# Filter rows of a spectral mixer: even rows read backwards by DMA instead of turned on TensorE

## The chip, the cores and the metric

The kernel runs on one core of a Trainium2 chip. The metric is the device time of one execution in microseconds, as the median of several runs. The engines named below are TensorE (PE, with its weight loads as PEld), VectorE (DVE), ScalarE (ACT), GpSimd (POOL, unused here) and SyncE (SP), whose instruction stream issues nearly all DMAs of this kernel.

## The reference

Two branches read the same `x` of shape (1, 2048, 512), and a gate mixes them.

```python
def _A_ref(x, w_r, w_i):                      # spectral filter
    X = rfft2(x)                              # over (2048, 512), 257 columns kept
    X = X * (w_r + 1j * w_i)                  # filter: 2048 x 257
    return irfft2(X, s=(2048, 512)).astype(bf16)

def _B_ref(x, w1, b1, w2, b2):                # MLP over the token axis
    h = layernorm(x)
    u = gelu(einsum("bsd,sf->bdf", h, w1) + b1)      # f = 1792
    y = einsum("bdf,fs->bds", u, w2) + b2
    return y.transpose(0, 2, 1)

g = sigmoid((x * gate_w).sum(-1))
return g * A + (1 - g) * B
```

Inputs, tables and output are bfloat16; sums are kept in float32 in PSUM.

## The kernel before

**The transform.** The 2048-point transform along the tokens is split by four: DVE adds and subtracts quarters of `x`, PE multiplies by cosine and sine tables (`ta`, lines 509 to 516), and ACT copies the result to the tile `X` in SBUF. A frequency index k from 0 to 255 sits on each partition, the even ones in half `lt` = 0 of the tiles and the odd ones in half `lt` = 1; the four blocks of 512 frequencies and the mirrored ones stand in the free dimension. DVE finishes the token transform (`radix4`, lines 538 to 571), PE transforms along the 512 columns (`fb`, lines 618 to 625), ACT copies to the tile `B` (line 628), and DVE multiplies by the filter (`mul`, line 777) and combines (lines 782 to 791). Then everything runs backwards: an inverse radix-4 step on DVE, the matmuls `i1` (lines 838 to 845), folds on DVE (lines 861 to 874), the matmuls `i3` (lines 913 to 917) and the folds per output tile (lines 937 to 941).

**The filter in SBUF.** The tile `W` has the shape [128, component, lt, e, slot, 258]: the component is real or imaginary, e is one of four blocks of 512 rows, slot 0 holds row 512e + k, and slot 1 holds the mirrored row 2048 - 512e - k. The mirrored rows run downwards in the source as the partition goes up. For the odd rows, DMAs read them downwards (line 425). For the even rows they are loaded upwards into a tile `wt` (lines 419 to 423), and PE turns the partitions round with a reversed identity `flip` as the weights (`wf`, line 706; line 716 does column 256); ACT copies the result into `W` (lines 710 and 719). The even row k = 0 is a special case with rows of its own. `wprep` (lines 726 to 730) halves one row and prepares the sums for the edge columns; it is the first instruction of DVE that needs all of both components of `W`.

**The MLP.** First layer: 14 column tiles of `w1` times 16 token tiles, matmul by matmul (`m1`, line 656), then a gelu on ACT (line 670). Second layer: 16 output tiles j with 14 matmuls each (`m2`, line 932). The weights of the first layer lie in `wa` and two `wb` buffers; those of the second layer (seven loads of 1 MB, line 889) take over these buffers when they are free. These matmuls fill PE wherever the transform has nothing for it.

**The order of the work.** Every step is a task with an engine, an estimated duration, a priority and, for a DMA, a number of bytes. A planner (class `Plan`, lines 170 to 233) plays the tasks through with these estimates: whenever an engine is free, it takes the ready task with the smallest priority number. For a task with bytes, lines 222 to 225 move a common DMA clock on:

```python
if best.nbytes:
    dma_free = max(dma_free, now + best.dur + 1.0) + best.nbytes / 350e3
    end = dma_free + 0.4
    clock[eng] = max(clock[eng], dma_free - 5.0)
```

The planned times serve for nothing but the order: each engine's instructions are emitted in it, and every engine, SP too, works through its own list strictly in that order. The real waits are semaphores between the instructions that touch the same data.

**The loads that matter here.** SP issues the first four column loads of `wb`, then the gate weights, `ld_W(0)` (18 DMAs), the second four loads of `wb`, `ld_W(1)` (18 DMAs), the inverse table `ti`, the table `tg`, and the loads of `w2`. A row of the filter is 257 values, 514 bytes.

Of the kernel before, what the change touches and what calls it, by code (L numbers as in the profile page):

```python
# [34 lines left out]

def make_tables():
# [10 lines left out]
    for r in range(4):  # L47
        s = 4 * p + r
        for n, k0 in enumerate((0, 2)):
            th = ang(s, k0 + 4 * np.arange(64), S)  # L50
            ta[:, r, n * 128:n * 128 + 64] = np.cos(th)
            ta[:, r, n * 128 + 64:n * 128 + 128] = -np.sin(th)
        ta[:, r, 64] = alt
# [5 lines left out]
        k = np.where(p < 64, 4 * p, 2 + 4 * (p - 64))  # L59
        o, w = ti_at(r)  # L60
        v = ti[:, o:o + w]
        if r % 2:
            sg = np.where(p < 64, 1.0, -1.0)[:, None]
# [6 lines left out]
            v[0, 2:4] = alt * (0.5 ** 0.5 if r == 1 else -(0.5 ** 0.5))  # L70
            th = ang(1 + 4 * (p ^ 96), s, S)
            v[:, 4] = -np.sin(th)
            v[:, 5] = np.cos(th)
            v[:, 6] = np.sin(th)
            ti[:, o:o + w] = v.reshape(P, w)
        else:
            s5 = np.append(s, 512)
            for lt, kk in enumerate((k, 1 + 4 * (p ^ 96))):
                th = ang(kk, s5, S)
                c, n = np.cos(th), -np.sin(th)  # L80
                if lt == 0:
                    n[0, 0:P] = 0.0 if r == 0 else -alt
# [4 lines left out]
    ti[0, 2816:2945] = np.append(alt, 1.0)  # L87
# [174 lines left out]
def kernel(  # L262
# [150 lines left out]
    def ld_W(comp):  # L413
        v = wsrc[comp].rearrange("(e c k) l -> c e k l", e=4, k=4)
        z = wsrc[comp].rearrange("(v u w) l -> w u v l", v=4, u=2)

        def emit():
            W, u = t["W"][:, comp], t["wt"][:, comp]
            dma(u[64:127, :, 0:257], v[65:128, :, 0, :])
            dma(u[0:64, :, 0:257], v[64:128, :, 2, :])  # L420
            dma(u[127:128, 0:2, 0:257], z[0:1, 1, 2:4, :])
            dma(u[127:128, 2, 0:257], wsrc[comp][1536:1537, :])
            dma(u[127:128, 3, 0:257], wsrc[comp][0:1, :])
            for e in range(4):
                dma(W[:, 1, e, 1, 0:257], v[:, 3 - e, 3, :].rearrange("(o i) l -> o i l", o=4)[:, ::-1])
# [150 lines left out]
    def sp0():  # L576
        V.tensor_copy(t["sp"][:], t["X"][:, 0, :, :, :, 0])
# [25 lines left out]
    add("DVE", 0.15, lambda: V.tensor_copy(t["X"][:, 0, :, :, :, 0], t["fx"][:]), reads=["fx"],  # L603
# [94 lines left out]
    for comp in range(2):  # L698
        for lt in (0,):
            for a in range(2):  # L700
                tag = ("fa", "fb")[a]

                def wf(comp=comp, lt=lt, a=a, tag=tag):
                    pw = t["pw", comp, lt, a] = ps([P, 2, L], F32, tag, 2)
                    for i in range(2):
                        T.matmul(pw[:, i], lhsT=t["flip"][:], rhs=t["wt"][:, comp, 3 - 2 * a - i, 0:L], start=True, stop=True)
                add("PE", mm(256, 256), wf, reads=[("wt", comp), "flip"], writes=[("pw", comp, lt, a)], prio=5, alloc=[tag])

                def wfe(comp=comp, lt=lt, a=a):
                    A.copy(t["W"][:, comp, lt, 2 * a:2 * a + 2, 1, 0:L], t["pw", comp, lt, a][:])  # L710
                add("ACT", act(512), wfe, reads=[("pw", comp, lt, a)], writes=[("W~", comp, lt)], prio=3, free=[tag])

    def wfn():
        pw = t["pwn"] = ps([P, 4, 2], F32, "fa", 2)
        for e in range(4):
            T.matmul(pw[:, e], lhsT=t["flip"][:], rhs=t["wt"][:, :, 3 - e, 256], start=True, stop=True)
    add("PE", mm(*[4] * 4), wfn, reads=[("wt", 0), ("wt", 1), "flip"], writes=["pwn"], prio=5, alloc=["fa"])
    wtk = [("W~", comp, 0) for comp in range(2)]
    add("ACT", 0.3, lambda: A.copy(t["W"][:, :, 0, :, 1, 256], t["pwn"][:].rearrange("p e k -> p k e")),
        reads=["pwn"], writes=wtk, prio=3, free=["fa"])  # L720

    pbk = [("pb", lt, e, c) for lt in range(2) for e in range(4) for c in range(2)]

    def wprep():
        W, pm = t["W"], t["wpm"]
        V.tensor_scalar_mul(W[0:1, :, 0, 0, :, 0:257], W[0:1, :, 0, 0, :, 0:257], 0.5)
# [4 lines left out]
    add("DVE", 0.8, wprep, reads=[], writes=[("W", 0), ("W", 1), "wpm"] + wtk, prio=1)  # L731


    for lt in range(2):
# [8 lines left out]
        if lt == 0:  # L743
            def nyq():
                pz = sb([1, 1280], F32, "X")
                na = pz[:, 0:1024].rearrange("p (i v l) -> p i v l", i=2, v=2)
                nn = t["nn"] = pz[:, 1024:1280].bitcast(BF16).rearrange("p (v l) -> p v l", v=2)
                wn, v = t["wn"], t["B"][0:1, 0, 0, 2:4, :]
# [4 lines left out]
                V.tensor_mul(nn[:, :, 0], t["c0"][0:1, 0, 0, 1, :], wn[:, 0, 0:257:256])  # L753
# [18 lines left out]
        for comp in range(2):  # L772
# [5 lines left out]
            add("DVE", tt(4096), mul, reads=["xs", ("W", comp), ("W~", comp, lt)], writes=[("pp", "st")[comp]], prio=pr)  # L778
# [236 lines left out]
```

## Time and profile before

| what | value |
|---|---|
| median of 3 runs | 134.28 us (133.79 to 134.64) |
| the profiled execution | 134.46 us, span 132.6 us, granted clock 1.0 |
| PE busy | 124.6 us, 94% of the span |
| DVE busy | 115.3 us, 87% |
| ACT busy | 80.5 us, 61% |
| DMA | 23.18 MB, 175 GB/s mean over the span |
| SP issues `ld_W(0)` | from 21.70 to 34.66 us |
| SP issues `ld_W(1)` | from 37.37 to 51.05 us |
| last `m1` matmul ends, first `m2` matmul starts | about 70.4 us |

The profile shows one execution. Times in it count from the start of the span; the 1.86 us between the span and the execution's time lie outside it. A group of instructions stands with its line, engine, tiles and mean duration; "idle before" is the time that an engine waited, with the instruction or DMA that released it. The DMA share is the mean busy share of the core's 16 DMA engines, so that 0.25 is the work of four of them.

### The profile page before, as it was taken

The page shows a single profiled execution, that of the slowest core. Times are in us where ns is not written, and L with a number is a line of the kernel's source. Part 1 is how long each engine was busy: PE and PEld are TensorE (multiplying, and loading weights), DVE is VectorE, ACT ScalarE, POOL GpSimd, SP SyncE. Part 2 cuts the span into 40 slices and gives each one's busy share as a digit, 9 for nine tenths or more (in the row PEclk, how much of TensorE's full clock was granted, in tenths as well). Part 3 has the DMA queues.
Part 4 walks back from the last instruction along what each step waited for, and adds up shares of the span by engine and source line. Part 5 has one row for each costly group of instructions (what it writes and reads, how often), then busy time and mean ns, then how long its engine had stood idle before and what let it go on. Part 6 is the DMA issues. An engine that isn't in the chain of part 4 may idle for free.

```text
span 132.6 us, 2193 instructions
## 1 busy us (share of the span) xinstructions
PE 124.6 (94%) x769; PEld 70.7 (53%) x783; DVE 115.3 (87%) x295; ACT 80.5 (61%) x155; POOL 0.2 (0%) x4
## 2 busy tenths in 40 slices
PE   6749999999999999999999999999999999999991
PEld 2234464545544566744445544556865766655590
DVE  2987999999999997389999999999598599999841
ACT  4036699999999999972222016235994857755200
POOL 0000000000000000000000000000000000000000
PEclk9999999999999999999999999999999999999999
DMA  4899999925499565999964930000000003034031
GB/s 133 245 370 394 393 380 371 321 60 134 90 309 342 96 134 131 337 373 413 421 253 72 420 146 2 0 2 5 0 0 0 5 0 158 23 135 161 2 119 40
DMA packets 17350, 23.18 MB, mean 175 GB/s; under 512 B 1446, under 2 KB 14780, under 8 KB 17340
## 3 DMA queue, kind: packets, MB, share of 16 engines
q1 hardware_dynamic: 16780, 22.39, 49.8%
q10 hardware_dynamic: 560, 0.66, 1.6%
q8 instruction: 6, 0.10, 0.3%
q14 instruction: 4, 0.03, 0.1%
HBM read 20.93 MB, written 2.10 MB: 174 GB/s over the span
## 4 chain that ended last, share of the span: by engine, by line
PE 80%; DVE 10%; DMA 6%; SPq 1%; issue 1%
PE acc L932 35%; PE acc L656 25%; DMA x<-in_A_x_dram 6%; DVE stats L462 4%; PE fb L656 3%; PE fa L838 1%; PE fb L838 1%; PE fa L624 1%; PE fb L624 1%; SPq L303 1%; DVE mv L463 1%; DVE gl L495 1%; DVE st L494 1%; PE fa L513 1%; DVE nmr L477 1%
## 5 line engine op out<-in xcount | busy, mean ns | idle before, releaser
L932 PE MATMUL acc<-gl,wb 128*128 128x512 bf16 (+1 forms) x123 | 30.5, 373 | 0.3
L656 PE MATMUL acc<-h,wb 128*128 128x512 bf16 x124 | 28.8, 379 | 0.2
L932 PE MATMUL acc<-gl,wa 128*128 128x512 bf16 (+1 forms) x94 | 23.2, 372 | 0.1
L932 PEld LDWEIGHTS <-wb 128*128 128x128 bf16 x144 | 14.9, 114 | 10.7 <-DMA wb<-in_B_w_dram 0.6
L952 ACT ACTIVATE x<-acc,ombb,omg 128x512 bf16<-128x512 f32 x14 | 10.7, 778 | 15.5 <-PE acc L932 15.4
L656 PEld LDWEIGHTS <-wb 128*128 128x128 bf16 x128 | 12.4, 97 | 13.5
L656 PE MATMUL acc<-h,wa 128*128 128x512 bf16 x62 | 16.8, 379 | 1.2 <-DVE stats L462 0.7
L932 PEld LDWEIGHTS <-wa 128*128 128x128 bf16 x108 | 11.7, 114 | 8.5
L656 PEld LDWEIGHTS <-wa 128*128 128x128 bf16 x96 | 9.1, 98 | 10.3 <-DMA wa<-in_B_w_dram 0.9
L670 ACT ACTIVATE gl<-acc,b1f 128x512 bf16<-128x512 f32 x12 | 8.5, 708 | 9.6 <-PE acc L656 9.6
L462 DVE BATCH_NORM_STATS2 stats<-x 128x6 f32<-128x512 bf16 x16 | 10.8, 673 | 2.8 <-DMA x<-in_A_x_dram 2.8
L519 ACT CAST X<-fa 128x512 bf16<-128x512 f32 x16 | 8.8, 583 | 3.9 <-PE fa L516 3.8
L486 ACT ACTIVATE h<-x,nmr,rstd 128x512 bf16<-128x512 bf16 x13 | 9.8, 805 | 1.2 <-DVE nmr L477 1.2
L684 ACT ACTIVATE x<-x 128x512 bf16<-128x512 bf16 x16 | 10.2, 672 | 0.0
L923 ACT ACTIVATE eo<-fa,g 128x512 bf16<-128x512 f32 x8 | 5.5, 688 | 6.7 <-DVE x L958 5.0
L656 PE MATMUL fb<-h,wa 128*128 128x512 bf16 x31 | 9.0, 379 | 0.0
L513 PE MATMUL fa<-rot,gl 128*128 128x256 bf16 x16 | 4.3, 272 | 2.1 <-DMA rot<-dft_ta 2.1
L353 PE MATMUL fa<-xp 128*128 128x512 bf16 x13 | 4.4, 514 | 1.2 <-DVE xp L314 1.2
L923 ACT ACTIVATE eo<-fb,g 128x512 bf16<-128x512 f32 x8 | 5.5, 686 | 0.0
L958 DVE TENSOR_TENSOR x<-x,eo 128x512 bf16<-128x512 bf16 x14 | 5.4, 418 | 0.0
L628 ACT CAST B<-fb 128x512 bf16<-128x512 f32 x8 | 5.2, 651 | 0.0
L628 ACT CAST B<-fa 128x512 bf16<-128x512 f32 x8 | 5.1, 639 | 0.0
(170 smaller groups left out, 227.3 us busy)
## 6 DMA issues: line engine op xcount, KB each, us to landing
wb<-in_B_w_dram SPq DMA_DIRECT2D x8, 512.0 KB
wb<-in_B_w_dram SPq DMA_DIRECT2D x4, 1024.0 KB
wa<-in_B_w_dram SPq DMA_DIRECT2D x3, 1024.0 KB
wa<-in_B_w_dram SPq DMA_DIRECT2D x3, 768.0 KB
x<-in_A_x_dram SPq DMA_DIRECT2D x3, 512.0 KB
out_dram<-x SPq DMA_DIRECT2D x3, 512.0 KB
rot<-dft_ti SPq DMA_DIRECT2D x1, 736.5 KB
rot<-dft_ta SPq DMA_DIRECT2D x4, 160.0 KB
```

The source lines that it names most:

```text
L462: V.bn_stats(out=t["stats"][:, j, :], in_=t["x"][:, j // 4, j % 4, :])
L486: add("ACT", act(512, 2), lambda j=j: A.activation(t["h"][:, j // 4, j % 4, :], t["x"][:, j // 4, j % 4, :], ActF.Identity, bias=t["nmr"][ ...
L513: T.matmul(pa[:, 1], lhsT=w(2), rhs=ta[:, 256:512], start=True, stop=False)
L519: add("ACT", act(512), lambda r=r, dq=dq: A.copy(t["X"][:, :, r, :, dq, :], t["pa", r, dq][:]), reads=[("pa", r, dq)], writes=[("X", r, dq ...
L628: A.copy(t["B"][:, lt, e, 2 * c:2 * c + 2, :].rearrange("p s (i b) -> p s i b", b=4), t["pb", lt, e, c][:].rearrange("p s b i -> p s i b"))
L656: T.matmul(t["u", ft][:], lhsT=w[:, j // 4, j % 4, c * P:(c + 1) * P], rhs=t["h"][:, j // 4, j % 4, :], start=(j == jorder[0]), stop=(j == ...
L670: gelus.append(add("ACT", act(512, 1), lambda ft=ft: A.activation(t["gl"][:, ft, :], t["u", ft][:], ActF.Gelu_apprx_tanh, bias=t["b1f"][:, ...
L684: A.activation(t["x"][:, q, r, :], t["x"][:, q, r, :], ActF.Copy, accum_out=t["glog"][:, 4 * q + r:4 * q + r + 1])
L923: A.activation(t["eo", j][:], t["i3", j][:], ActF.Copy, scale=t["g"][:, j:j + 1])
L932: T.matmul(t["y", j, n][:, cs], lhsT=w[:, o, 512 * q + r:512 * q + 512:4], rhs=t["gl"][:, ft, cs], start=(ft == 0), stop=(ft == NFT - 1))
L952: A.activation(tbuf(j).rearrange("p h d -> p (h d)"), t["y", j, 0][:], ActF.Identity, bias=t["ombb2"][:, j:j + 1], scale=t["omg"][:, j:j + 1])
L958: V.tensor_add(o, o, t["eo", j][:])
```

## The change

The mirrored even rows are read downwards by DMA straight into `W`. For this the even frequencies are renumbered: partition 32q + i now holds k = 250 + 2q - 8i (modulo 256), that is one residue modulo 8 in each run of 32 partitions. The tables `ta` and `ti` follow, and row k = 0 moves from partition 0 to partition 96. The tile `wt`, the turning matmuls and their copies go. Per component there are now 20 DMAs in `ld_W`: for each o of four an even load in four downward runs, a mirrored load of 32 partitions (31 for o = 3), a single-row load, the odd load in four downward runs as before, and the odd forward load as before. The two DMAs that put the special rows over partition 96 become a task of their own with a later priority. The planner's figures for the loads change with it, and the tile `ze` gets memory of its own instead of that of `h`.

```diff
+KE = (250 + 2 * (np.arange(P) // 32) - 8 * (np.arange(P) % 32)) % 256
...
         def emit():
-            W, u = t["W"][:, comp], t["wt"][:, comp]
-            dma(u[64:127, :, 0:257], v[65:128, :, 0, :])
-            dma(u[0:64, :, 0:257], v[64:128, :, 2, :])
-            dma(u[127:128, 0:2, 0:257], z[0:1, 1, 2:4, :])
-            dma(u[127:128, 2, 0:257], wsrc[comp][1536:1537, :])
-            dma(u[127:128, 3, 0:257], wsrc[comp][0:1, :])
-            for e in range(4):
-                dma(W[:, 1, e, 1, 0:257], v[:, 3 - e, 3, :].rearrange("(o i) l -> o i l", o=4)[:, ::-1])
+            W, src = t["W"][:, comp], wsrc[comp]
+            tiny_ = [(W[96:97, 0, 1:3, 1, 0:257], z[0:1, 0:2, 3, :]), (W[96:97, 0, 0, 1, 0:257], src[0:1, :]),
+                     (W[96:97, 0, 3, 1, 0:257], src[1280:1281, :]), (t["wn"][96:97, comp, 0:257], src[1024:1025, :])]
             for o in range(4):
+                dma(W[:, 0, o, 0, 0:257], src[512 * o + 2:512 * o + 258, :].rearrange("(i q z) l -> q z i l", q=4, z=2)[:, 0, ::-1])
+                dma(W[32 * o + o // 3:32 * o + 32, 0, :, 1, 0:257], y[32 + o // 3:64, ::-1, 6 - 2 * o, :])
+                dma(*tiny_[o])
+                dma(W[:, 1, o, 1, 0:257], v[:, 3 - o, 3, :].rearrange("(o i) l -> o i l", o=4)[:, ::-1])
                 dma(W[32 * o:32 * o + 32, 1, :, 0, 0:257], v[96 - 32 * o:128 - 32 * o, :, 1, :])
-            dma(W[1:64, 0, :, 0, 0:257], v[1:64, :, 0, :])
-            dma(W[64:128, 0, :, 0, 0:257], v[0:64, :, 2, :])
+
+        def special():
             for i in range(2):
-                dma(W[0:1, 0, 2 * i:2 * i + 2, 0, 0:257], z[0:1, i, 0:2, :])
-            dma(t["wn"][:, comp, 0:257], wsrc[comp][1024:1025, :])
-        return emit
+                dma(t["W"][96:97, comp, 0, 2 * i:2 * i + 2, 0, 0:257], z[0:1, i, 0:2, :])
+        return emit, special

     for comp in range(2):
-        add("SP", 9.0 - 2 * comp, ld_W(comp), writes=[("W", comp), ("wt", comp)], prio=17 + 8 * comp, nbytes=300000, after=[a0])
+        emit, special = ld_W(comp)
+        add("SP", 8.0, emit, writes=[("W", comp)], prio=17 + 8 * comp, nbytes=1100000, after=[a0])
+        add("SP", 1.0, special, writes=[("W", comp)], prio=24 + 5.5 * comp, nbytes=4112)
...
-                T.matmul(pa[:, 0, :, 0:64], lhsT=w(0), rhs=ta[:, 0:128], start=True, stop=True)
-                T.matmul(pa[:, 0, :, 64:128], lhsT=w(1), rhs=ta[:, 128:256], start=True, stop=True)
+                T.matmul(pe[:, :, :, 1], lhsT=w(0), rhs=ta[:, 0:128], start=True, stop=True)
+                T.matmul(pe[:, :, :, 0], lhsT=w(1), rhs=ta[:, 128:256], start=True, stop=True)
...
-                        T.matmul(pw[:, i], lhsT=t["flip"][:], rhs=t["wt"][:, comp, 3 - 2 * a - i, 0:L], start=True, stop=True)
-                    A.copy(t["W"][:, comp, lt, 2 * a:2 * a + 2, 1, 0:L], t["pw", comp, lt, a][:])
-            T.matmul(pw[:, e], lhsT=t["flip"][:], rhs=t["wt"][:, :, 3 - e, 256], start=True, stop=True)
-    add("ACT", 0.3, lambda: A.copy(t["W"][:, :, 0, :, 1, 256], t["pwn"][:].rearrange("p e k -> p k e")),
...
-        V.tensor_scalar_mul(W[0:1, :, 0, 0, :, 0:257], W[0:1, :, 0, 0, :, 0:257], 0.5)
+        V.tensor_scalar_mul(W[96:97, :, 0, 0, :, 0:257], W[96:97, :, 0, 0, :, 0:257], 0.5)
...
-                dma(t["s9"][0:8], t["B"][0:1, 0].rearrange("p e (c v) l -> p (e c) (v l)", c=2))
+                dma(t["s9"][0:8], t["B"][96:97, 0].rearrange("p e (c v) l -> p (e c) (v l)", c=2))
...
-                        t["ze"] = sb([P, 2, 2, 2, 2, L], BF16, "h")
+                        t["ze"] = sb([P, 2, 2, 2, 2, L], BF16, "ze")
```

More of the change, by code (lines that the diff above doesn't have):

```diff
@@ L48, in make_tables @@
         s = 4 * p + r
-        for n, k0 in enumerate((0, 2)):
-            th = ang(s, k0 + 4 * np.arange(64), S)
+        for n in range(2):
+            kk = KE.reshape(2, 2, 32)[:, 1 - n].reshape(64)
+            th = ang(s, kk, S)
             ta[:, r, n * 128:n * 128 + 64] = np.cos(th)
             ta[:, r, n * 128 + 64:n * 128 + 128] = -np.sin(th)
-        ta[:, r, 64] = alt
+        ta[:, r, 96] = alt
         th = ang(s, 1 + 4 * (p ^ 96), S)
@@ L57, in make_tables @@
         ta[:, r, 512:640] = -np.cos(th)
-        k = np.where(p < 64, 4 * p, 2 + 4 * (p - 64))
+        k = KE
         o, w = ti_at(r)
@@ L62, in make_tables @@
         if r % 2:
-            sg = np.where(p < 64, 1.0, -1.0)[:, None]
+            sg = np.where(k % 4 == 2, -1.0, 1.0)[:, None]
             th = ang(k, s, S)
@@ L69, in make_tables @@
             v[:, 3] = -sg * np.sin(th)
-            v[0, 2:4] = alt * (0.5 ** 0.5 if r == 1 else -(0.5 ** 0.5))
+            v[96, 2:4] = alt * (0.5 ** 0.5 if r == 1 else -(0.5 ** 0.5))
             th = ang(1 + 4 * (p ^ 96), s, S)
@@ L81, in make_tables @@
                 if lt == 0:
-                    n[0, 0:P] = 0.0 if r == 0 else -alt
+                    n[96, 0:P] = 0.0 if r == 0 else -alt
                 u = v[:, 256 * lt:256 * lt + 256]
@@ L86, in make_tables @@
                     u[:, P] = c[:, P] if lt == 0 else -n[:, P]
-    ti[0, 2816:2945] = np.append(alt, 1.0)
+    ti[96, 2816:2945] = np.append(alt, 1.0)
     tb = np.zeros((P, 3, 4, 64))
@@ L322, in alloc_first @@
         t["W"] = sb([P, 2, 2, 4, 2, WL], BF16, "W")
-        t["wn"] = sb([1, 2, WL], BF16, "wn")
+        t["wn"] = sb([P, 2, WL], BF16, "wn")
         t["ta"] = sb([P, 4, 640], BF16, "rot")
-        t["wt"] = sb([P, 2, 4, WL], BF16, "wt")
         t["wpm"] = sb([P, 2, 2, 4, 2], F32, "wpm")
@@ L414, in ld_W @@
         v = wsrc[comp].rearrange("(e c k) l -> c e k l", e=4, k=4)
+        y = wsrc[comp].rearrange("(e c k) l -> c e k l", e=4, k=8)
         z = wsrc[comp].rearrange("(v u w) l -> w u v l", v=4, u=2)
         def emit():
[L418 to L425 removed]
+            W, src = t["W"][:, comp], wsrc[comp]
+            tiny_ = [(W[96:97, 0, 1:3, 1, 0:257], z[0:1, 0:2, 3, :]), (W[96:97, 0, 0, 1, 0:257], src[0:1, :]),
+                     (W[96:97, 0, 3, 1, 0:257], src[1280:1281, :]), (t["wn"][96:97, comp, 0:257], src[1024:1025, :])]
             for o in range(4):
+                dma(W[:, 0, o, 0, 0:257], src[512 * o + 2:512 * o + 258, :].rearrange("(i q z) l -> q z i l", q=4, z=2)[:, 0, ::-1])
+                dma(W[32 * o + o // 3:32 * o + 32, 0, :, 1, 0:257], y[32 + o // 3:64, ::-1, 6 - 2 * o, :])
+                dma(*tiny_[o])
+                dma(W[:, 1, o, 1, 0:257], v[:, 3 - o, 3, :].rearrange("(o i) l -> o i l", o=4)[:, ::-1])
                 dma(W[32 * o:32 * o + 32, 1, :, 0, 0:257], v[96 - 32 * o:128 - 32 * o, :, 1, :])
[L428 to L429 removed]
+        def special():
             for i in range(2):
[L431 to L433 removed]
+                dma(t["W"][96:97, comp, 0, 2 * i:2 * i + 2, 0, 0:257], z[0:1, i, 0:2, :])
+        return emit, special
     for comp in range(2):
[L436 removed]
+        emit, special = ld_W(comp)
+        add("SP", 8.0, emit, writes=[("W", comp)], prio=17 + 8 * comp, nbytes=1100000, after=[a0])
+        add("SP", 1.0, special, writes=[("W", comp)], prio=24 + 5.5 * comp, nbytes=4112)
         if comp == 0:
@@ L511, in fa @@
                 ta = t["ta"][:, r, :]
+                pe = pa[:, 0].rearrange("p c (h o i) -> p c h o i", h=2, o=2)
                 w = lambda k: t["xf", r][:, k, dq * P:(dq + 1) * P]
@@ L576, in sp0 @@
     def sp0():
-        V.tensor_copy(t["sp"][:], t["X"][:, 0, :, :, :, 0])
+        V.tensor_copy(t["sp"][:], t["X"][:, 0, :, :, :, 96])
     dk = [("D", r) for r in range(4)]
@@ L602 @@
                dk + ([] if lt else ["sp"]), [("Z", lt, 0), ("Z", lt, 1)], pr, False)
-    add("DVE", 0.15, lambda: V.tensor_copy(t["X"][:, 0, :, :, :, 0], t["fx"][:]), reads=["fx"],
+    add("DVE", 0.15, lambda: V.tensor_copy(t["X"][:, 0, :, :, :, 96], t["fx"][:]), reads=["fx"],
         writes=[("Z", 0, 0), ("Z", 0, 1)], prio=3.1)
@@ L696 @@
     add("SP", 0.2, ld_ti, writes=["ti"], prio=28, nbytes=754176, after=[pl.last_w["pa", r, dq] for r in range(4) for dq in range(4)])
[L698 to L709, printed above, removed]
-                    A.copy(t["W"][:, comp, lt, 2 * a:2 * a + 2, 1, 0:L], t["pw", comp, lt, a][:])
[L711 to L718, printed above, removed]
-    add("ACT", 0.3, lambda: A.copy(t["W"][:, :, 0, :, 1, 256], t["pwn"][:].rearrange("p e k -> p k e")),
-        reads=["pwn"], writes=wtk, prio=3, free=["fa"])
     pbk = [("pb", lt, e, c) for lt in range(2) for e in range(4) for c in range(2)]
@@ L730, in wprep @@
         V.tensor_sub(pv[1], ends[1][:, :, 0], ends[1][:, :, 1])
-    add("DVE", 0.8, wprep, reads=[], writes=[("W", 0), ("W", 1), "wpm"] + wtk, prio=1)
+    add("DVE", 0.8, wprep, reads=[], writes=[("W", 0), ("W", 1), "wpm"], prio=1)
     for lt in range(2):
@@ L744, in nyq @@
             def nyq():
-                pz = sb([1, 1280], F32, "X")
+                pz = sb([P, 1280], F32, "X")[96:97]
                 na = pz[:, 0:1024].rearrange("p (i v l) -> p i v l", i=2, v=2)
                 nn = t["nn"] = pz[:, 1024:1280].bitcast(BF16).rearrange("p (v l) -> p v l", v=2)
-                wn, v = t["wn"], t["B"][0:1, 0, 0, 2:4, :]
+                wn, v = t["wn"][96:97], t["B"][96:97, 0, 0, 2:4, :]
                 for i in range(2):
@@ L752, in nyq @@
                 V.tensor_add(nn[:, 1], na[:, 1, 1], na[:, 0, 0])
-                V.tensor_mul(nn[:, :, 0], t["c0"][0:1, 0, 0, 1, :], wn[:, 0, 0:257:256])
+                V.tensor_mul(nn[:, :, 0], t["c0"][96:97, 0, 0, 1, :], wn[:, 0, 0:257:256])
             add("DVE", 3 * d1(512) + 0.1, nyq, reads=bk + [("W", 0), ("W", 1), ("c0", 0)] + pbk, writes=["nn"], prio=0.5)
@@ L777, in mul @@
                 V.tensor_mul(o, xs, w)
-            add("DVE", tt(4096), mul, reads=["xs", ("W", comp), ("W~", comp, lt)], writes=[("pp", "st")[comp]], prio=pr)
+            add("DVE", tt(4096), mul, reads=["xs", ("W", comp)], writes=[("pp", "st")[comp]], prio=pr)
         def comb(lt=lt):
@@ L817 @@
         if lt == 0:
-            add("SP", 0.5, lambda: dma(t["B"][0:1, 0].rearrange("p e (c v) l -> p (e c) (v l)", c=2), t["s8"][:]),
+            add("SP", 0.5, lambda: dma(t["B"][96:97, 0].rearrange("p e (c v) l -> p (e c) (v l)", c=2), t["s8"][:]),
                 reads=["s8"], writes=[("T", 0, 0), ("T", 0, 1)], prio=0, nbytes=8192)
```

## The prediction

> **What bounds the kernel now.** I read the page first, then the chain of work that ended last, then DVE's and SP's instructions in order of time.
>
> ```profile
> PE 124.6 (94%) x769; PEld 70.7 (53%) x783; DVE 115.3 (87%) x295; ACT 80.5 (61%) x155; POOL 0.2 (0%) x4
> ...
> PE   6749999999999999999999999999999999999991
> ...
> DVE  2987999999999997389999999999598599999841
> ...
> PE 80%; DVE 10%; DMA 6%; SPq 1%; issue 1%
> ```
>
> PE is fed from about 13 us to 129.7 us and carries 80% of the chain. Taking work from PE pays only while nothing that PE waits for gets later. DVE is the near rival: it has one dip, in the slice from 53 to 56 us. Its list there and at the end:
>
> ```profile
> 51.60 0.24 DVE L603 CAST X<-fx 128x32 bf16<-128x32 f32 x1
> 52.52 0.42 DVE L726 TENSOR_SCALAR W<-W 1x1028 bf16<-1x1028 bf16 x1 [0.68 <-DMA W<-in_A_w_i_dram]
> ...
> 56.20 0.17 DVE L740 CAST c<-B 128x8 f32<-128x8 bf16 x1 [2.18 <-ACT B L628]
> ...
> 62.10 2.27 DVE L777 TENSOR_TENSOR xp<-xp,W 128x4096 bf16<-128x4096 bf16 x1
> ```
> ```profile
> 125.20 0.42 DVE L958 TENSOR_TENSOR x<-x,eo 128x512 bf16<-128x512 bf16 x1
> 126.65 0.75 DVE L970 SCALAR_TENSOR_TENSOR x<-acc,omg,x 128x512 bf16<-128x512 f32 x1 [1.04 <-PE acc L932]
> ```
>
> L726 is the first reader of the whole filter and waits for the last row of `W`. The matmul-sized product L777 starts at 62.10, and from there DVE runs on to 125.62 with gaps of only 1.17, 0.39, 0.32 and 1.45 us, each behind a matmul and a copy that themselves follow DVE. Then it waits 1.04 us for PE. So a delay of L777 of some 3 us or more comes out at the end.
>
> **What goes.** Four pairs of turning matmuls and the four small ones:
>
> ```profile
> 35.83 0.38 PE L706 MATMUL fa<-wt,flip 128*128 128x256 bf16 x2
> 50.07 0.24 PE L716 MATMUL fa<-wt,flip 128*128 128x2 bf16 x4
> ```
>
> The next instruction starts 0.21 us after a pair (36.04) and 0.11 after the small ones (50.18), so 4 x 0.215 + 0.11 = 0.97 us of PE go, all on the chain. ACT loses 4 x 0.48 + 0.35 = 2.3 us; it waits elsewhere (9.6 us for L656), and the copies to `B` that release L740 start behind L603 all the same: nothing gained. Cost at nothing: the `fa` output in runs of 32 instead of 64 (L624, which writes every other run of 64, takes the same 272 ns as the contiguous L513; a dearer write would show on 32 matmuls of 0.06 us); partition 96 for 0 (same shapes); `ze` in its own memory (L853 first writes it at 91.16, `h` was last read at 70.4).
>
> **What comes: the loads.** The same bytes go in 22 DMAs per component for 18. What matters is how they spread over the 16 DMA engines. In these stretches of 1 us, the last two columns are DMA share and GB/s:
>
> ```profile
> 28.00:29.00 1.00, 1.00 (x7) 0.46 (x5) 1.00 (x4) 1.00 (x2) 0.00 (x0) 1.00 0.13 37
> 29.00:30.00 1.00, 1.00 (x6) 0.43 (x5) 1.00 (x3) 0.98 (x2) 0.00 (x0) 1.00 0.13 31
> 31.00:32.00 1.00, 1.00 (x10) 0.60 (x8) 1.00 (x4) 1.00 (x3) 0.00 (x0) 1.00 0.80 176
> 46.00:47.00 1.00, 1.00 (x12) 0.80 (x10) 1.00 (x3) 1.00 (x4) 0.00 (x0) 1.00 0.20 53
> 50.00:51.00 1.00, 1.00 (x10) 0.49 (x8) 1.00 (x3) 1.00 (x3) 0.00 (x0) 1.00 0.75 148
> ```
>
> The odd loads in four downward runs (issued 27.81 to 29.54 and 44.73 to 45.88) never fill more than a fifth to a third of the engines; the forward loads of 32 partitions behind them reach 0.8. Four runs, about four of sixteen engines: the outermost count of a load decides how many engines share it. A row costs an engine 514 B x 16 x share / rate: 29 ns at 28 to 29 us, 37 at 31 to 32, 42 at 50 to 51. I take 35.
>
> Rows on the first engine, per component: a load in four runs 32, a load of 32 partitions by four rows 8. Before: 4 x 32 + 4 x 8, 64 to 88 for the four large even loads, some 6 single rows: about 240, or 8.4 us. As a check, from the third run load on (about 46.2) 2 x 32 + 32 + 44 rows x 35 ns end at 51.1, and the DMA share falls to nothing at 51.5. After: 8 x 32 + 4 x 8 + 3 x 8, some 5 single rows, and the mirrored load of 31 partitions, 124 rows. The trace has no such count. If it spreads over all engines it puts 8 rows (0.3 us) on the first; if 31, which splits evenly over no number up to 16 but one, goes to one engine, 124 rows (4.3 us). I take the one engine, since four runs went to four, and keep both ends. That makes 441 rows, 15.4 us, against 325, 11.4 us.
>
> The Trainium skill, DMA: Bandwidth & Descriptors, section "Why a DMA increments its semaphore by 16 and not by 1", says that a DMA from SP runs on the largest number of engines up to 16 that divides the slowest dimension of both sides, the lowest-numbered ones. By that rule 31 partitions run on one engine, and the trace's 0.13 to 0.20 for four runs agrees. By it alone the sum would be the one taken here.
>
> **The order behind them.** SP runs eight DMAs ahead: the second and third run loads of component 1 waited 1.6 us each for the third and fourth `wb` load, eight issues before. So SP follows the slow engine. The planner puts the special rows of component 1 late: they become ready 12.54 us after that `ld_W` starts (8 + 1 + 3.14 + 0.4 by lines 222 to 225), SP is free after 8, and `ti`, `tg` and the first `w2` load pass first and keep SP until 12.76. `wprep` reads these rows, so it waits behind 1.95 MB. That small loads queue so:
>
> ```profile
> 71.91 0.76 SPq L303 DMA_DIRECT2D s<-B  x1
> ```
> ```profile
> SPq L303 <- DMA s<-B: 5.3, 1, 5.3
> ```
>
> 8 KB issued at 71.91 behind two `w2` loads were waited for until 78.6. In DVE's list I keep `wprep` ahead of the second L740: its planned ready time moves from 48.8 to 53.3, while the copies to `B`, with one gelu now let in between, are planned ready at 53.6 (53.3 before).
>
> **The sum.** First engine: the first `wb` loads drain at 26.0 (307 GB/s at 25 to 26, 120 after); component 0 to 41.4; four `wb` loads, 131 KB each engine at 383/16 GB/s, 5.5, to 46.9; component 1 to 62.3; `ti` 1.9, `tg` 0.4, `w2` 2.5 (418 to 430 GB/s), to 67.1; landing 1.1 (data ended 51.4, L726 began 52.52): L726 at **68.2**. Behind it on DVE: L726 to L730 0.87, L740/L741 0.15, two blocks L758 to L763 1.06, L750 to L753 2.17, L769/L770 2.27: 6.5. L777 starts at 74.7, 12.6 later than 62.10. DVE's stretch ends at 138.2; L970 then takes 0.67 + 0.40 + 0.28 + 0.35 = 1.70: 139.9 against 130.09 before, **+9.8 us**. PE agrees: `i1` starts 12.6 after about 90.0, some 2.1 us of `m2` having moved ahead of it (1.1 planned, 1.0 freed), and ends 39.1 - 2.1 later: 139.6 against 129.7. On the way PE also waits for `w2`, whose loads lie in the same queue (first due at 69.5, there at 68.2, the next ones 2.5 to 2.7 us apart), up to 9 us before 86, all before `i1` waits for DVE. So 134.46 + 9.8 = 144.3 against the profiled execution, 0.18 above the median: **144.1 us**. With 29 or 42 ns a row, L726 comes at 63.0 or 74.4: 139 to 150.
>
> **Rivals.**
> (a) The 31 partitions spread. Then SP's issue bounds: 2 + 2 + 2 more issues of 0.57 before `ti`, so `ld_W(1)` ends near 54.3 for 51.05; `ti` to landed `w2` took about 7 us from 51.15 (1.95 MB by the rates after it): L726 at 61, L777 at 67.5, +5.4, less the slack of 2.77 used above: +2.6, 137 us. For it: the 63-row loads show no queue of a one-engine kind. Against it: 31 is not 63.
> (b) Faster or equal: the special rows land by 57, because SP's list or the engines let them past. Then DVE loses at most 1.4 us in its dip, which ends at 56.20 anyway, and PE's 0.97 us come out: 133.3, within 1%. Against it: SP's in-order list and the 6.7 us of the 8 KB load. This side ends where L726 comes at about 58.4: every us later costs one.
> (c) DVE does L769/L770 ahead of `wprep`: 2.3 us less than (a) or the forecast, 135 or 142. It turns on 0.3 us of planned time.
> (d) The change doesn't do what it says: a spread of the run loads over all engines would cut the load stage below 9 us each; the shares above speak against it. It would be (b).
>
> **Numbers.** One engine for 31 partitions 0.60 (with c inside); (a) 0.21; (b) and (d) 0.19, of which 0.07 faster by over 1%. Range 135.5 to 150: the forecast's own 139 to 150, and (a). Faster by over 1% 0.07, within 1% 0.12, slower 0.81; 1% is about what a measurement of this kernel can tell from no change (the runs shown span 0.6%).
>
> **What would show it.** Right: no L706 and L716; stretches of the load stages at a DMA share of about 0.06 for some 4 us each; SP waiting several us for `W`; L726 idle ten us or more, released by a DMA of `W`; PE waiting for `w2` after 69 us; L777 near 75. With (a): no share near 0.06, L726 near 61. With (b): L726 before 58 and L970 waiting for PE as now. Wrong would be a `W` that lands in time with DVE late for another cause, or late rows that DVE's tail absorbs.

## Result, and the profile after

| | time, median (lowest to highest) | ratio, 95% interval | profiled execution | its span |
|---|---|---|---|---|
| before | 134.25 us (133.79 to 135.18) | 1 | 134.46 | 132.6 |
| after | 143.80 us (143.55 to 145.44) | 1.073 [1.067, 1.079] | 144.58 | 142.4 |

The changed kernel is 9.5 us slower; 144.1 us was forecast. Medians take in all executions; the ratios, here and below, leave out those more than 1.5% above the fastest of the same kernel. First the page of the changed kernel: engine totals, the slices of PE, of DVE and of the granted clock, and the chain that ended last.

```profile
PE 128.8 (90%) x771; PEld 70.3 (49%) x771; DVE 115.3 (81%) x295; ACT 78.6 (55%) x150; POOL 0.2 (0%) x4
...
PE   6959999999999999999724999999599999999991
...
DVE  3969999999999960001999999999987959999991
...
PEclk9999999999999999999995599999999999999999
...
DMA 31%; DVE 25%; PE 24%; SPq 14%; issue 3%
```

PE carried 80% of the chain before and carries 24% now; DMA, DVE and SP's queue have taken its place. DVE's one dip of before has become five weak slices of 3.56 us each, three of them empty, and two slices show the matmul clock at half. DVE's instructions around the dip, in order of time (start, duration, what it is, idle time before it and what ended that), with line numbers of the changed kernel: L707 is `wprep` (L726 before), L758 the first product (L777 before).

```profile
52.20 0.18 DVE L695 TENSOR_SCALAR omg<-g 128x16 f32<-128x16 f32 x1 [0.45 <-ACT g L691]
67.21 0.43 DVE L707 TENSOR_SCALAR W<-W 1x1028 bf16<-1x1028 bf16 x1 [14.55 <-DMA W<-in_A_w_i_dram]
...
74.08 2.29 DVE L758 TENSOR_TENSOR xp<-xp,W 128x4096 bf16<-128x4096 bf16 x1
```

DVE waits 14.55 us for the last row of `W`, and the first product starts 11.98 us later than before. The end of DVE's list (L951 was L970):

```profile
137.47 1.14 DVE L951 SCALAR_TENSOR_TENSOR x<-acc,omg,x 128x512 bf16<-128x512 f32 x2
...
139.55 0.35 DVE L951 SCALAR_TENSOR_TENSOR x<-fb,omg,x 128x128 bf16<-128x128 f32 x1 [0.43 <-PE fb L913]
```

It ends at 139.90, against 130.09 before (129.74 and 0.35): 9.8 us. What kept `W` away is in SP's list of the second component's loads (start, duration of the group, number of DMAs):

```profile
51.73 2.50 SPq L307 DMA_DIRECT2D W<-in_A_w_i_dram  x5
54.27 1.79 SPq L307 DMA_DIRECT2D wn<-in_A_w_i_dram  x1
56.11 1.08 SPq L307 DMA_DIRECT2D W<-in_A_w_i_dram  x2
57.29 0.37 SPq L307 DMA_DIRECT2D rot<-dft_ti  x1
57.71 0.41 SPq L307 DMA_DIRECT2D tg<-dft_tg  x1
58.23 0.38 SPq L307 DMA_DIRECT2D wa<-in_B_w_dram  x1
58.66 2.75 SPq L307 DMA_DIRECT2D W<-in_A_w_i_dram  x2
```

The last two `W` loads, the special rows, are issued behind `ti`, `tg` and the first `w2` load, and the second of them waits 1.5 us more, for a load of `W`, before it is issued. Its issue, and SP's waits for `W` (total, times, longest):

```profile
60.83 0.59 SPq L307 DMA_DIRECT2D W<-in_A_w_i_dram  x1
```
```profile
SPq L307 <- DMA W<-in_A_w_i_dram: 1.5, 1, 1.5
```

What it waits for is the mirrored load of 31 partitions, issued at 53.77, eight DMAs earlier: the trace also records when each engine's share of a DMA lands, and this load has one share, which landed at 60.81. Right behind it SP issued `wn`, and that issue takes 1.79 us, where the same `wn` issue took 0.41 us before. Stretches of the load stage (busy time of each engine, then the clock, and in the last two columns the mean busy share of the 16 DMA engines and GB/s):

```profile
36.50:37.50 1.00, 1.00 (x7) 0.44 (x5) 1.00 (x1) 1.00 (x4) 0.00 (x0) 1.00 0.06 15
...
55.00:56.00 1.00, 1.00 (x8) 0.52 (x6) 0.00 (x0) 1.00 (x4) 0.00 (x0) 1.00 0.27 77
56.25:57.25 1.00, 1.00 (x6) 0.47 (x5) 0.00 (x0) 0.99 (x2) 0.00 (x0) 1.00 0.07 20
```

One engine of sixteen is 0.0625. Late in both components one engine works alone for a good microsecond, and some four work (0.27) before that in the second. The stretch ends at about 57.5 because the other engines begin with `ti`; the lone engine has not yet finished its rows then, as the landing at 60.81 shows.

PE's waits for `w2` in the same kernel (start, duration, idle time before it), and the windows behind them (the clock is the third number from the end):

```profile
72.08 0.62 PE L913 MATMUL acc<-gl,wa 128*128 128x512 bf16 x2 [1.67 <-DMA wa<-in_B_w_dram]
74.63 0.69 PE L913 MATMUL acc<-gl,wb 128*128 128x512 bf16 x2 [1.93 <-DMA wb<-in_B_w_dram]
77.19 1.04 PE L913 MATMUL acc<-gl,wb 128*128 128x512 bf16 x2 [1.87 <-DMA wb<-in_B_w_dram]
...
102.12 0.22 PE L823 MATMUL fa<-rot,B 128*128 128x129 bf16 x1 [1.74 <-DMA B<-s]
```
```profile
74.00:75.00 1.00, 0.37 (x2) 0.15 (x2) 0.97 (x2) 0.00 (x0) 0.00 (x0) 1.00 1.03 410
75.00:76.00 1.00, 0.33 (x2) 0.00 (x0) 1.00 (x1) 0.00 (x0) 0.00 (x0) 0.53 1.01 401
...
81.00:82.00 1.00, 1.00 (x4) 0.41 (x3) 1.00 (x1) 0.00 (x0) 0.00 (x0) 0.56 0.08 33
82.00:83.00 1.00, 1.00 (x7) 0.49 (x5) 1.00 (x3) 0.00 (x0) 0.00 (x0) 1.00 0.00 0
```

So there are two late arms. **DVE's arm** is the filter's last row; **PE's arm** is `w2`, 5.47 us of waits, followed by some 7 us at a clock of 0.50. PE still had to wait 1.74 us at the first inverse matmul (L823) for DVE's side, whose last piece a small DMA (`B<-s`) brings, so DVE's arm was the later of the two, by 1.74 us.

Two formulas are used below. DVE's arm ends at 134.3 + (start of the first product - 62.10) - 2.77, with the slack of 2.77 us that the prediction used. PE's arm ends at 134.3 + the waits for `w2` + half of the time that PE is busy at a clock of 0.5. For the changed kernel they give 143.5 and 134.3 + 5.47 + 2.5 = 142.3 us (5.13 us busy at a mean clock of 0.51 between 75 and 82). Both are estimates from these traces: the later arm comes within 1.1 us of the profiled execution in the changed kernel and in runs 1, 2, 4, 5 and 6.

### The profile page after: what moved, and what is told of

Read it like the earlier page. It is cut to its first block, busy times and chain, and to the rows that moved or that the text cites. A ratio compares the mean times of both kernels' runs of the same rounds, so it can differ in the third digit from the quotient of the medians.

```text
span 142.4 us, 2187 instructions
## 1 busy us (share of the span) xinstructions
PE 128.8 (90%) x771; PEld 70.3 (49%) x771; DVE 115.3 (81%) x295; ACT 78.6 (55%) x150; POOL 0.2 (0%) x4
## 4 chain that ended last, share of the span: by engine, by line
DMA 31%; DVE 25%; PE 24%; SPq 14%; issue 3%
PE acc L913 17%; DMA wa<-in_B_w_dram 16%; SPq L307 14%; DMA wb<-in_B_w_dram 6%; DMA gw<-in_gate_w_dram 5%; DMA W<-in_A_w_i_dram 5%; DVE xp L758 3%; DVE st L758 3%; DVE xp L763 2%; DVE st L558 2%; DVE B L770 2%; DVE xp L750 2%; DVE xp L764 2%; DVE xp L751 2%; PE fb L819 1%
## 5 line engine op out<-in xcount | busy, mean ns | idle before, releaser
L913 PE MATMUL acc<-gl,wb 128*128 128x512 bf16 (+1 forms) x128 | 32.5, 383 | 3.8 <-DMA wb<-in_B_w_dram 3.8
L913 PE MATMUL acc<-gl,wa 128*128 128x512 bf16 (+1 forms) x96 | 24.9, 389 | 1.7 <-DMA wa<-in_B_w_dram 1.7
L707 DVE TENSOR_SCALAR W<-W 1x1028 bf16<-1x1028 bf16 x1 | 0.4, 430 | 14.5 <-DMA W<-in_A_w_i_dram 14.5
L356 PE MATMUL fa<-xp 128*128 128x512 bf16 x13 | 5.7, 631 | 1.2 <-DVE xp L318 1.2
```

The lines of the kernel that those rows point to most:

```text
L913: T.matmul(t["y", j, n][:, cs], lhsT=w[:, o, 512 * q + r:512 * q + 512:4], rhs=t["gl"][:, ft, cs], start=(ft == 0), stop=(ft == NFT - 1))
```

## Experiments

Each time stands against runs of the kernel before on the same chip (medians 134.2 to 134.7).

**1. The load of 31 partitions as 15 + 16.** By the rule of the Trainium skill that the prediction cites (DMA: Bandwidth & Descriptors, section "Why a DMA increments its semaphore by 16 and not by 1"), 15 partitions run on fifteen engines and 16 on sixteen; the trace of this run agrees, with fifteen and sixteen shares landing.

```
-  dma(W[32*o + o//3:32*o + 32, 0, :, 1, 0:257], y[32 + o//3:64, ::-1, 6 - 2*o, :])
+  if o < 3: dma(W[32*o:32*o + 32, 0, :, 1, 0:257], y[32:64, ::-1, 6 - 2*o, :])
+  else:
+      dma(W[97:112, 0, :, 1, 0:257], y[33:48, ::-1, 0, :])
+      dma(W[112:128, 0, :, 1, 0:257], y[48:64, ::-1, 0, :])
```

> The change with one edit: the mirrored load of 31 partitions is issued as two loads, of 15 and of 16 partitions. Theory A (the 31-row load runs on one DMA engine, fills its queue and holds SP and the special rows): the two issues of wn, 1.96 and 1.79 us behind it, fall to about 0.5, the special rows no longer wait 1.5 us for W, no stretch is left at a DMA share of 0.06 to 0.07; the first reader of W (L707 in the changed kernel, at 67.2) comes at 63 to 64.5, time 140 to 141.5. Theory B (only the number of SP's issues counts): one more issue per component, 144 to 145.

Measured: 140.43 us, ratio 1.042 [1.033, 1.052]. SP's list and DVE's:

```profile
54.25 0.27 SPq L307 DMA_DIRECT2D wn<-in_A_w_i_dram  x1
```
```profile
64.33 0.43 DVE L711 TENSOR_SCALAR W<-W 1x1028 bf16<-1x1028 bf16 x1 [11.95 <-DMA W<-in_A_w_i_dram]
```

The `wn` issue is back at 0.27 us, no stretch near 0.06 is left, and `wprep` comes 2.9 us earlier, although there is one DMA more. The single engine is shown, and is worth 3.4 us of the 9.5 by the medians (4.1 by the ratios, give or take 1.5). The 2.9 us give no price of a row: the load of component 0 is split too, and SP reaches component 1 at 40.88 where it was 42.40. The first product is at 71.19, which gives 140.6 for DVE's arm; PE waited 4.08 us for `w2` and was busy for 5.94 us at half the clock, which gives 141.4 (the profiled execution took 141.49).

**2. The special rows ahead of `ti`, `tg` and `w2`.** In the plan, the three wait for the special rows' task; nothing else is changed.

```
-  load("tg", [P, 642], BF16, tabs["tg"], 164352, prio=29)
+  load("tg", [P, 642], BF16, tabs["tg"], 164352, prio=29).deps.add(special_of_component_1)
   ... and `after=[special_of_component_1]` for ld_ti and w2alloc
```

> The change with the special rows of component 1 planned ahead of ti, tg and the w2 loads. Theory A (two arms: the late filter holds DVE, the late w2 loads hold PE, and both end about level): the first reader of W comes near 60 instead of 67.2, but PE still waits for w2 between 70 and 82, and the time falls only to 141.5 to 143. Theory C (the place of the special rows in the queue is the whole cause): DVE's tail alone decides, 135 to 136.5.

Measured: 141.96 us, ratio 1.048 [1.037, 1.059].

```profile
61.34 0.43 DVE L707 TENSOR_SCALAR W<-W 1x1028 bf16<-1x1028 bf16 x1 [8.96 <-DMA W<-in_A_w_i_dram]
68.13 2.29 DVE L758 TENSOR_TENSOR xp<-xp,W 128x4096 bf16<-128x4096 bf16 x1
```
```profile
70.67 0.62 PE L913 MATMUL acc<-gl,wa 128*128 128x512 bf16 x2 [0.96 <-DMA wa<-in_B_w_dram]
73.22 0.62 PE L913 MATMUL acc<-gl,wa 128*128 128x512 bf16 x2 [1.93 <-DMA wa<-in_B_w_dram]
75.79 1.04 PE L913 MATMUL acc<-gl,wb 128*128 128x512 bf16 x2 [1.94 <-DMA wb<-in_B_w_dram]
```

The first product comes 5.95 us earlier than in the changed kernel, but the time falls by 1.84 us only by the medians, and by 3.3 us, give or take 1.7, by the ratios. DVE's arm alone would have given 137.6. PE's arm gives 134.3 + 4.83 + 3.0 = 142.1. This fits the theory of two arms, and not that of the queue place alone; that the gain is just the 1.74 us by which DVE's arm had been the later is within the noise, not shown.

**3. The four-run loads read upward.** The filter rows then stand in the wrong order inside the runs.

```
-  src[512*o + 2:512*o + 258, :].rearrange("(i q z) l -> q z i l", q=4, z=2)[:, 0, ::-1]
+  src[512*o + 2:512*o + 258, :].rearrange("(i q z) l -> q z i l", q=4, z=2)[:, 0]
   (and the odd rows' [:, ::-1] left out)
```

> The loads in four runs are read upwards instead of downwards, four runs all the same; the order of the filter rows inside each run is left wrong. Theory A (the number of runs decides, not the direction): DMA share during these loads stays at 0.2 to 0.3, time 143.8 within 0.7. Theory D (reading backwards is what is slow): the load stages shorten by some 3 us each, time 138 to 140.

Measured: 140.68 us, ratio 1.046 [1.036, 1.056]; `wprep` at 63.34. This run doesn't isolate the direction. The odd loads, read upward, were issued in 0.35 us instead of 0.55 and landed in sixteen shares instead of four, so they no longer ran on four engines; the even ones kept their four shares and their 0.58 to 0.60 us. That reading backwards by itself costs nothing is supported only for the issue of the even loads.

**4. All large loads as 32 partitions by 4 rows, upward, with the split of run 1.** Again the filter rows stand in the wrong order.

```
-  dma(W[:, 0, o, 0, 0:257], src[...].rearrange("(i q z) l -> q z i l", q=4, z=2)[:, 0, ::-1])
+  dma(W[32*o:32*o + 32, 0, :, 0, 0:257], y[o//3:32 + o//3, :, (2 + 2*o) % 8, :])
-  dma(W[:, 1, o, 1, 0:257], v[:, 3 - o, 3, :].rearrange("(o i) l -> o i l", o=4)[:, ::-1])
+  dma(W[32*o:32*o + 32, 1, :, 1, 0:257], v[32*o:32*o + 32, ::-1, 3, :])
```

> As the run with 15 and 16 partitions, and the four-run loads replaced by as many loads of 32 partitions by four rows read upwards; the order of the filter rows is left wrong. Theory of the prediction (the first DMA engine's 35 ns a row times 441 rows bounds the load stages): the stages fall to some 6 us of DMA each, first reader of W near 60, 136 to 138. Theory B (SP's issues bound the stages once the 31-row load is split): little beyond the split run, first reader of W 62.5 to 64, 139.5 to 141.

Measured: 139.33 us, ratio 1.032 [1.023, 1.041]; `wprep` at 61.63, first product at 68.46. With no large load on few engines any more, SP still reaches `ti` only at 53.19 (51.15 before, 57.29 after the change): 21 issues, most of 0.27 to 0.47 us, and their waits for `wb` hold it. So the loads on few engines, their longer issues included, account for 4.1 us of SP's delay; the other 2.0 stay here, where the added issues and the special rows of component 0 are what is left, not told apart. DVE's arm is 134.3 + 6.36 - 2.77 = 137.9; PE idled 2.97 us for DVE's side, and around that it was busy for 2.6 us at a clock of 0.50, which makes 139.2.

**5. Split and special rows first (runs 1 and 2 together).**

> The changed kernel with the 31-partition load as 15 + 16 partitions, and with the special rows of component 1 ahead of ti, tg and the first w2 load. Theory (two arms: SP's pace decides when the filter's last row lands for the DVE, and when w2 is issued for PE; the end is the later arm): the split alone brought wprep to 64.33, the order alone to 61.34, each some 3 us by its own; together wprep at 58 to 59.5, w2 issued some 3 us earlier than with the order alone (141.96), PE still some 2 us short of w2: 138 to 139.8. Rival (one arm, the DVE chain alone sets the end): wprep 8.5 us earlier than in the changed kernel, so 135 to 136. Rival (the two edits overlap, both free the same stretch): no faster than the split alone, 140 to 141.

Measured: 136.60 us, ratio 1.015 [1.008, 1.022], better than the theory and close to its first rival. DVE, PE, and a window behind PE's wait:

```profile
57.03 0.43 DVE L711 TENSOR_SCALAR W<-W 1x1028 bf16<-1x1028 bf16 x1 [5.14 <-DMA W<-in_A_w_i_dram]
63.82 2.29 DVE L762 TENSOR_TENSOR xp<-xp,W 128x4096 bf16<-128x4096 bf16 x1
```
```profile
72.10 0.83 PE L917 MATMUL acc<-gl,wb 128*128 128x512 bf16 x2 [1.93 <-DMA wb<-in_B_w_dram]
```
```profile
73.00:74.00 1.00, 1.00 (x3) 0.30 (x2) 0.96 (x3) 0.00 (x0) 0.00 (x0) 0.50 0.99 397
```

The first product is only 1.72 us later than before the change, inside the slack. What is left is PE's arm: 134.3 + 1.93 + 1.7 = 137.9, 1.3 us more than the median (0.9 more than the profiled execution). Two small edits to the loads and their order give back 7.2 of the 9.5 us.

**6. As 5, with `ti` and `tg` behind the first five `w2` loads.** Only the two tables' places in the plan are changed (their `prio` from 28 and 29 to 36.5 and 36.4).

> As the run with the split and the special rows first (136.6), and the tables ti and tg (0.92 MB) are issued behind the first five w2 loads instead of ahead of them. Two arms: PE was short of w2 once, 1.93 us, in that run; the two tables take 2.2 us at 418 GB/s and 0.9 us of issues on SP, so w2 lands some 2 to 3 us earlier and PE's wait goes, and with it the stretch of halved clock behind it (granted clock 0.60 and 0.55 between 72 and 76). wprep stays at 57. If the wait of PE and the halved clock set the end: 134.3 to 135.5. If the DVE chain set it (its first product stood at 63.82, 1.72 us later than before the change): 136 to 136.8, no gain.

Measured: 135.46 us, ratio 1.009 [1.006, 1.012].

```profile
63.78 2.29 DVE L762 TENSOR_TENSOR xp<-xp,W 128x4096 bf16<-128x4096 bf16 x1
```
```profile
72.36 0.62 PE L917 MATMUL acc<-gl,wb 128*128 128x512 bf16 x2 [1.14 <-DMA wb<-in_B_w_dram]
```
```profile
73.00:74.00 1.00, 1.00 (x6) 0.55 (x5) 0.97 (x3) 0.00 (x0) 0.00 (x0) 1.00 1.00 400
```

DVE's start is the same as in run 5, and the time falls by 1.1 us with PE's wait down from 1.93 to 1.14 us and no halved clock behind it. That fits PE's arm as what set run 5; by the formula it is now 135.4. The times alone don't show it, since the intervals of the two ratios overlap.

**7. As 6, with the first butterfly ahead of `wprep` on DVE.** The `wprep` task is planned behind `bfly` of the first half.

> As the run before it, and the DVE does the first butterfly ahead of wprep, in the 5 us in which it waits for the filter. B is there at about 56, so the butterfly ends at 59, wprep, the small products and the line at 128 follow, and the first product of 4096 starts at 62.2 to 63, against 63.82 and against 62.10 before the change. If the DVE chain sets the end: 0.8 to 1.6 us below the run without this, 134 to 135. If PE alone sets it: as the run without this. If every arm is back where it was, the 0.97 us of turning matmuls shows: 133.3.

Measured: 136.03 us (133.90 to 139.26), ratio 1.005 [1.000, 1.010].

```profile
56.09 0.17 DVE L717 CAST c<-B 128x8 f32<-128x8 bf16 x1 [3.56 <-ACT B L637]
57.15 0.17 DVE L718 CAST c<-B 128x8 f32<-128x8 bf16 x1 [0.89 <-ACT B L637]
...
63.98 2.29 DVE L763 TENSOR_TENSOR xp<-xp,W 128x4096 bf16<-128x4096 bf16 x1
```

The first product didn't come earlier. The filter had landed at 57.0 in run 6, and `B` is complete at 57.15 here: the two meet, so the order of their first readers is indifferent. 62.2 to 63 was expected from a `B` at 56.

**8 to 10. The four second `wb` loads issued from ScalarE instead of SP**: in the kernel of run 5, in the changed kernel, and in the kernel before as a control.

```
-  dma(t["wb", k][:, q], w1v[:, q, :, FA + D*k:FA + D*(k + 1)])
+  dma(t["wb", k][:, q], w1v[:, q, :, FA + D*k:FA + D*(k + 1)], A if k else None)
   (the four loads become tasks of ScalarE with a place of their own in the plan, and `wprep` is planned
    behind the token transform of the even half, and `omg`)
```

> As the run with the split and the special rows first, and the four second wb loads are issued from ScalarE instead of SP, so SP loses four issues of 0.6 us and their waits between the components. Theory (SP's pace sets both arms): component 1 ends on SP near 50 to 52, ti and w2 are issued where they were before the change, wprep no later than 56, PE never short of w2: 133 to 135; if all is hidden, the 0.97 us of turning matmuls shows and it is 133.3. Rival (the data path itself is full, the pace of SP only mirrors it): component 1 no earlier than 54, 137.5 to 139.5.

> The changed kernel with nothing but the four second wb loads issued from ScalarE instead of SP. Theory (SP's pace): SP reaches the end of component 1 some 4 to 5 us earlier (57.2 to about 52.5), wprep at 62 to 63.5, w2 issued 4 us earlier: 138 to 140. Theory of the prediction (the first engine works off 441 rows a component, whatever else stands in the queue): component 1 lands no earlier than 57.5, wprep as now: 142.5 to 144.

> Control: the kernel before with the four second wb loads issued from ScalarE. If issuing from ScalarE costs or gains nothing by itself, 134.2 plus or minus 0.8, as before; if the filter's arrival also set the end before the change, 131 to 133; if ScalarE is held up by the loads, 136 or more.

Measured: 140.71 us (ratio 1.049 [1.042, 1.056]), 145.64 us (1.085 [1.078, 1.092]) and the control 139.93 us (1.042 [1.035, 1.049]). The edit itself costs 5.7 us, so the first two say little of SP's pace. The control's waits (total, times, longest) show ScalarE standing still for a load that it issued itself (the fourth load is issued only when one of its earlier ones has landed), and PE standing still behind it:

```profile
ACT L673 <- DMA wb<-in_B_w_dram: 4.3, 1, 4.3
```
```profile
36.22 0.37 PE L513 MATMUL fa<-rot,gl 128*128 128x256 bf16 x1 [3.97 <-ACT X L519]
```

PE waits 3.97 us for ScalarE's copy of a result to `X` and is busy for 4.94 us at a clock of 0.50 between 34.3 and 41.2; by PE's formula that is 6.4 us, near the 5.7 measured. Later DVE also waits 5.48 us for a copy to `B`. SP's pace stays untested by these runs.

**11. The kernel before without its turning.** The same loads bring the rows straight to `W`, where they stand in the wrong order; the matmuls L706 and L716 and their evacuations are gone.

```
-  W, u = t["W"][:, comp], t["wt"][:, comp]
+  W = t["W"][:, comp]
+  u = W[:, 0, :, 1]
   (and the loops with wf, wfe and wfn left out; `wprep` is planned behind the token transform of the even half)
```

> The kernel before without its turning matmuls and their evacuations: the rows that were turned are loaded straight to their place with the same loads, so they stand there in the wrong order. Nothing else is changed. It measures the gain by itself. Prediction's term: 0.97 us of PE on the chain that sets the end, 133.3. If PE's order has slack there: 134.2, as before. If ScalarE's 2.3 us or the earlier wprep count too: 132 to 132.8.

Measured: 134.08 us, ratio 0.9997 [0.996, 1.003]. A gain of 0.97 us would be 0.993, outside the interval.

**12. The kernel before with each of the eight large turning matmuls done three times.**

```
-  T.matmul(pw[:, i], lhsT=t["flip"][:], rhs=t["wt"][:, comp, 3 - 2*a - i, 0:L], start=True, stop=True)
+  for _ in range(3):
+      T.matmul(pw[:, i], lhsT=t["flip"][:], rhs=t["wt"][:, comp, 3 - 2*a - i, 0:L], start=True, stop=True)
```

> The kernel before with each of its eight turning matmuls of 256 columns done three times in a row, the same result written again. A pair ends 0.22 us after the pair before it (0.77 us of busy time for four pairs by the groups of before), so 16 more matmuls are 1.5 to 1.8 us of PE. If PE's turning lies on the path that sets the end: 135.8 to 136.1, ratio 1.011 to 1.013. If it lies in slack, as the run without turning says (ratio 0.9997): 134.3, ratio below 1.004.

Measured: 135.49 us, ratio 1.009 [1.006, 1.012]: 1.2 us for some 1.5 to 1.8 us of added matmuls. More turning costs most of its time; less turning gained nothing that could be measured. The two don't fit one price, and why is open. Run 11's profiled execution had a granted clock of 0.85 between 10 and 20 us, but it took 134.97 us, and only two of the twelve executions were granted less than the full clock, so this doesn't hide a gain in the median.

## Why the prediction was right

The time (144.1 against 143.8), the sign and the two places (`wprep` at 67.21 for 68.2, the first product at 74.08 for 74.7) came out, and runs 1, 2 and 5 show that the causes were the ones named. By its steps:

- **One engine for 31 partitions: right.** Shares of 0.06 and 0.07, and 2.9 us of `wprep` with the split. The landings agree: one share for the 31 partitions, four for a load in four runs, sixteen for a load of 32 partitions. The rule of the Trainium skill, DMA: Bandwidth & Descriptors, section "Why a DMA increments its semaphore by 16 and not by 1", holds here for 31 partitions (0.0625 expected) and for four runs (0.27, against 0.25). Two signs were smaller than foretold: the stretch near 0.06 lasts a good microsecond in each component and not some 4, and SP waits for `W` once, 1.5 us.
- **35 ns a row, and 62.3 for the second component's end: nearly right.** The share of the 31-partition load landed 4.07 us after the last share of the run load ahead of it (60.81 and 56.74), and 3.68 us in the first component (40.73 and 37.05): 33 and 30 ns for each of the 124 rows. In windows of 0.25 us the engine, alone at work, moved 19 to 21 GB/s, 24 to 27 ns a row; with `ti` on all engines it was slower. Of the packets that began between 59.25 and 60.25, 24 are rows of `W` (under 2 KB, less the two under 512 B), nearly all of them the lone engine's, since the others' last shares of the filter landed between 58.7 and 60.1:

```profile
DMA packets 80, 0.33 MB, mean 331 GB/s; under 512 B 2, under 2 KB 26, under 8 KB 80
```

The last row of the second component began at about 61.1, and the last share of its loads landed at 61.92. Whether the first engine or SP set the pace before the 31 partitions isn't told apart: SP began a round of loads every 2.6 us (48.01, 50.62, 53.19), and the even loads landed 2.9 and 2.7 us apart (51.15, 54.08, 56.74).

- **SP's order: right.** The special rows were issued behind `ti`, `tg` and the first `w2` load, just so, and run 2 brings `wprep` 5.9 us earlier.
- **4.8 us for 1.97 MB at 418 to 430 GB/s, and 1.1 for landing: nearly right.** From the last row at 61.1 to the last special rows at 66.4 it took 5.3 us, and 0.8 more to `wprep`. The last shares landed at 63.54 (`ti`), 63.98 (`tg`), 66.90 (`w2`) and 67.19 (special rows). The engines were busy, but with rows of `W` and tables among the data they moved less than the rate taken:

```profile
58.00:59.00 1.00, 1.00 (x6) 0.44 (x5) 0.00 (x0) 0.00 (x0) 0.00 (x0) 1.00 0.96 245
...
61.00:62.00 1.00, 1.00 (x6) 0.46 (x5) 0.00 (x0) 0.00 (x0) 0.00 (x0) 1.00 0.97 274
...
64.00:65.00 1.00, 1.00 (x6) 0.48 (x5) 0.00 (x0) 0.00 (x0) 0.00 (x0) 1.00 0.96 316
```

So each station of the sum lies within some 1.2 us of the trace. `wprep` came 1.0 us before the sum's 68.2, the operations behind it took 6.9 us for 6.5, and the tail absorbed 2.2 us for 2.77; that these cancel, and +9.8 us came out to the tenth, is luck.

- **DVE's tail with some 3 us of slack: right.** The first product 11.98 us later makes 9.8 us at DVE's end, 2.2 us absorbed. Its chain was the later arm, as the sum had it.
- **PE short of `w2` "up to 9 us before 86, all before `i1` waits for DVE": right in kind.** It was 5.47 us of waits, all before 78, and the halved clock on top, which was not foreseen. That made PE's arm almost as late as DVE's, so that undoing DVE's alone (run 2) pays 1.8 us by the medians where the forecast's sum would give 6.
- **0.97 us of PE for the turning: not found** in run 11, though run 12 shows that more of it would cost. The term is about a tenth of the change.
- **Rival (a)**, SP's issues as the bound, is half true: in run 4, in which no large load runs on few engines, `wprep` and the first product stand where (a) had them (61.63 for 61, 68.46 for 67.5), and the run still ends 4.6 us above the kernel before, where (a) gave 2.7, having no halved clock in it. Both causes pull in the same direction. **Rival (c)** did not come: `wprep` stayed ahead of the butterfly. What the other order is worth was tried only where filter and `B` arrive together (run 7), and there it is nothing.

None of the versions beats the kernel before: the best, runs 6 and 7, end 0.5 to 0.9% above it. The change trades about 1 us of matmuls, which doesn't show when it goes, for loads that use fewer engines and more issues of a queue on which two chains wait.

## What to carry to other kernels

Before turning rows by DMA, count for each load how many engines its outermost dimension feeds and how many rows the busiest one gets, and look at what stands behind it in the same queue: here 31 partitions instead of 32, and two loads of 1 KB behind 2 MB of tables and weights, made 7 of the 9.5 us. When two engines wait on one queue, cost both arms before undoing one, since the gain ends where the other begins. Follow a slow engine to the landing of its last row: the stretch in which it works alone ends when other loads begin, which can be long before it is done.

## What had not been expected of the hardware

- **The clock after short waits.** After a single PE wait of 1.93 us (run 5) the granted clock was 0.50 from 72.4 to 75.7; after three waits of 1.67 to 1.93 us it was 0.50 for some 7 us; after one of 1.14 us (run 6) it stayed at 1.00. In run 5 wait and dip together thus cost nearly twice the wait. The length of one wait doesn't decide: a wait of 2.06 us that ended at 7.71 in the kernel before, and the one of 1.74 us before 102.12 in the changed kernel, were followed by no dip, while run 11's dip from 9.5 to 12.9 came with a wait of 1.22 us. Each dip that ended before the run did lasted 3.4 or 6.8 us in these traces. The Trainium skill, TensorE: Matmul & The Clock Gate, section "Part 1: The HAM clock gate (the "warmup" mystery)", tells of the half rate after at least one idle window of about 3.4 us. The half rate agrees; here a single wait of 1.93 us was enough in run 5.
- **The issue behind a one-engine load.** SP's next issue took 1.79 and 1.96 us behind the load of 31 partitions, and 0.27 and 0.28 us behind the two loads of 15 and 16. Why it takes so long is not shown.
- **Issues differ with the form.** In the second component, SP spent 0.58 us on an even load in four runs, 0.48 on a mirrored load, 0.29 on a single row, 0.55 on an odd load in four runs and 0.48 on a forward load: 9.5 us for four rounds.
- **Issuing from a working engine.** Four loads moved to ScalarE cost the kernel before 5.7 us, through a stop of 4.3 us on ScalarE, behind which PE waited 3.97 us.
